# SwiGLU gate by one ScalarE function instead of tangent and a VectorE pass, with scores grouped by four, in a Linformer attention + feed-forward kernel

## The chip, the cores and the metric

The kernel runs on one core of a Trainium2 chip. TensorE (PE) multiplies matrices into PSUM, VectorE (DVE), ScalarE (ACT) and GpSimd (POOL) work on tiles, SyncE (SP) only issues DMAs here. The metric is the device time of one execution in microseconds (us); lower is better. The kernel before took 548.34 us, the median of three runs (547.98 to 548.58).

## The reference

Eight batches, eight heads, 1024 tokens, head size 64. Keys and values are first projected along the sequence from 1024 to 64 rows (E and F), then comes ordinary attention over those 64; its output, 512 wide per token, goes through a gated feed-forward block with 1536 inner columns:

```
k_proj = einsum('ks,bhsd->bhkd', E, k)
v_proj = einsum('ks,bhsd->bhkd', F, v)
attn = softmax(q @ k_proj^T / sqrt(64))
x = (attn @ v_proj)                # tokens x 512
g = x @ w_gate
silu = g * (1 / (1 + exp(-g)))
out = (silu * (x @ w_val)) @ w_out
```

## The kernel before

Tokens are taken in 16 chunks of 512 (two per batch, `c` = 2 * batch + half). A chunk has 12 steps `f`, one for each 128 inner columns. A step is two calls:

- `f_g` (L531): four 128x512 matmuls into a PSUM bank "gps" (two banks take turns), then ScalarE's tangent of half of it into the SBUF tile `th`.
- `f_v` (L537): four matmuls into a bank "vps" (two banks), then two VectorE passes: L541 makes `s1` = (th + 1) * gate, L546 makes `hT` = 0.5 * s1 * value, in bf16. Since x * sigmoid(x) = 0.5 * x * (1 + tanh(x / 2)), this is silu(gate) * value.

The output product of a finished chunk runs during the next chunk: from chunk 1 on as seven half-size products (`f_m`, L666; six 128x256 matmuls each, two products p), with sums of `hT` halves made on POOL and DVE (`h_sum`, L590) and of the results (`m_34`, `m_52`, `m_16`, `m_7`). Chunk 0 uses plain products (`f_y`, L552).

Attention of a batch is made in eight units `u` of 128 tokens by four heads pairwise, while the previous batch's feed-forward runs:

- `u_S` (L354): four 128x128 score matmuls into a bank "sc", then the exponent on ScalarE (L372) into `ee` (four buffers).
- `u_R` (L390): row sums and reciprocals on DVE. `u_N` (L398): normalising on POOL (L409).
- From batch 1 on a DMA on SP's queue transposes four units' weights at once (`u_AD`, L346), as q was before (`u_TD`). Batch 0 transposes on PE instead (`u_T`, `u_A`), with ScalarE or DVE copying the result out of PSUM.
- `u_PVt` (L457) or, for batch 0, `u_PV` (L444) multiplies by the projected values; copies into `xT` feed `f_g` and `f_v`.

The order is written out by hand. The main loop over all 192 steps `t` runs `f_g`, slot 2t, `f_v`, the list `late[t]` (output products and sums), slot 2t + 1. `place(b)` (L725) fills the slots of batch b, relative to s0 = 48 * (b - 1); batch 0's second half is filled at L926 to L931. Each engine follows its own queue in that order and waits on semaphores. Scores take the banks of `psa` ("a", two of them); while c < 2 a third bank ("z") takes part in turns (`bank`, L153). Two units on one slot follow each other on PE with nothing in between.

In the general branch (L774), which runs only when the row sums are out of bounds, the maximum is subtracted first; it does not run here.

```
for t in range(NIT):
    f_g(c, f, i)
    run_slot(2 * t)
    f_v(c, f, i)
    for fn, *a in late.pop(t, ()):
        fn(*a)
    run_slot(2 * t + 1)
```

Of the kernel before, what the change touches and what calls it, by code (L numbers as in the profile page):

```python
# [9 lines left out]
AF = mybir.ActivationFunctionType  # L10
ALU = mybir.AluOpType
AX = mybir.AxisListType
BF16 = mybir.dt.bfloat16
FP32 = mybir.dt.float32
# [8 lines left out]
P = 128  # L23
# [5 lines left out]
CW = 512  # L29
# [10 lines left out]
def kernel(  # L40
# [19 lines left out]
    nc = tc.nc  # L60
    scale = 1.0 / float(D) ** 0.5
# [8 lines left out]
    fw = ctx.enter_context(tc.tile_pool(name="fw", bufs=3))  # L70
# [26 lines left out]
    kb, vb, qb, xT, hT = {}, {}, {}, {}, {}  # L97
# [409 lines left out]
    gp = {}  # L507
# [3 lines left out]
    def f_mm(c, f, w, i=None):  # L511

        if i != 1:


            where = "y" if (c, f, w) == (0, 2, 0) else "gv"[w]
            half[c, f, w] = bank(where, [P, CW], FP32, where + "ps")
        ps = half[c, f, w]
        x = xT[divmod(c, CH)]
        ts = slice(0, CW) if i is None else slice(256 * i, 256 * (i + 1))  # L520
        for kt in range(NKT):
            nc.tensor.matmul(  # L522
                out=ps[:, ts],
                lhsT=(wg, wv)[w][:, kt, f * P : (f + 1) * P],
                rhs=x[:, kt, ts],
                start=(kt == 0),
                stop=(kt == NKT - 1),
            )
        return ps

    def f_g(c, f, i=None):  # L531
        ps = f_mm(c, f, 0, i)
        th = fw.tile([P, CW], FP32, name="th", tag="th")
        nc.scalar.activation(out=th[:], in_=ps[:], func=AF.Tanh, scale=0.5)  # L534
        gp[0] = (ps, th)

    def f_v(c, f, i=None):  # L537
        ps = f_mm(c, f, 1, i)
        g, th = gp.pop(0)
        s1 = fw.tile([P, CW], FP32, name="s1", tag="s1")  # L540
        nc.vector.scalar_tensor_tensor(  # L541
            out=s1[:], in0=th[:], scalar=1.0, in1=g[:], op0=ALU.add, op1=ALU.mult
        )
        if f == 0:
            hT[c] = h_pool.tile([P, NFT, CW], BF16, name="hT", tag="hT")
        nc.vector.scalar_tensor_tensor(  # L546
            out=hT[c][:, f, :], in0=s1[:], scalar=0.5, in1=ps[:], op0=ALU.mult, op1=ALU.mult
        )

    yy = {}  # L550

# [170 lines left out]
    def put(s, fn, *a):  # L722
        slots[s].append((fn, a))

    def place(b):  # L725
        s0 = 48 * (b - 1)
        if b == 1:
            put(22, u_TD, 1, 0)
            put(29, u_K1, 1)
            put(32, u_KT, 1)  # L730
            put(40, u_V1, 1)
            sa = (35, 36, 37, 38, 41, 42, 43, 44)
            put(41, u_AD, 1, 0)
            put(30, u_TD, 1, 1)
            put(47, u_AD, 1, 1)
            put(46, u_PVt, 1, 0, (0, 1), ("aa", "av"))
        else:
            if b == 2:
                put(s0 + 10, u_KV, b)
            else:  # L740
                put(s0 + 8, u_KV, b, "kv", (0, H), "v")
            put(s0 + (13 if b == 2 else 11), u_KT, b)
            put(s0 + (9 if b == 2 else -6), u_TD, b, 0)
            put(s0 + (11 if b == 2 else -4), u_TD, b, 1)
            sa = [s0 + j for j in ((17, 18, 22, 23, 27, 30, 33, 36) if b == 2 else (14, 17, 20, 23, 26, 29, 32, 35))]
            put(sa[3] + 4, u_AD, b, 0)
            put(sa[7] + 4, u_AD, b, 1)
            put(s0 + 44, u_PVt, b, 0, (0, 1), ("aa", "yz"))
        for j in range(NJ):
            put(sa[j], u_S, b, j)  # L750
            put(sa[j] + 1, u_R, b, j)
            put(sa[j] + 1, u_N, b, j)
        put(s0 + (68 if b == 1 else 56), u_PVt, b, 1, (0, 1), ("aa", "yz"))

    def run_slot(s):
# [18 lines left out]
    def general():  # L774
# [6 lines left out]
        with tc.For_i(0, B) as turn, tc.manual_schedule():  # L781
            turn_of.append(turn)
            b = 0
            load_k(b)
            load_v(b)
            u_KV(b)
            u_KT(b)
            for ch in range(CH):
                c = CH * b + ch
                load_q(b, ch)  # L790
                for u in range(4 * ch, 4 * ch + 4):
                    u_T(b, u)
                    u_S(b, u)
                    u_R(b, u)
                    u_N(b, u)
                    u_A(b, u)
                u_PVt(b, ch, (0, 1), ("aa", "yz"))
                for f in range(NFT):
                    f_g(c, f)
                    f_v(c, f)  # L800
                for m in (1, 2, 5, 6, 7):
                    h_sum(c, m, 0, HF, nc.vector)
                for n in range(14):
                    f_m(c, n)

    with tc.manual_schedule():
# [3 lines left out]
        for i in range(2):  # L810
            nc.scalar.dma_start(
                out=kraw[i][:],
                in_=k[0, 2 * i : 2 * i + 2].rearrange("h (p j) d -> p h (j d)", j=NJ),
# [111 lines left out]

        for i, u in enumerate(range(4, 8)):  # L926
            put((12, 12, 13, 14)[i], u_T, 0, u)
            put(13 + i, u_S, 0, u)
            put(14 + i, u_R, 0, u)
            put(14 + i, u_N, 0, u)  # L930
            put((17, 18, 20, 21)[i], u_A, 0, u, nc.scalar)  # L931
        put(19, u_PV, 0, 1, 0)
        put(20, u_PV, 0, 1, 1)
# [5 lines left out]
        for b in range(1, B):  # L939
            place(b)  # L940
        for b in range(2, B):
            s0 = 48 * (b - 1) - (20 if b == 3 else 24)
            at = (43, 43, 44, 45) if b == 2 else (s0, s0 + 2, s0 + 4, s0 + 6)
# [31 lines left out]
        for t in range(NIT):  # L975
            c, f = divmod(t, NFT)
            ring["wide"] = c < 2
            i = 1 if t < 2 else None
# [6 lines that stand above are left out]
# [34 lines left out]
```

## Time and profile before

| what | value |
|---|---|
| median of three runs | 548.34 us |
| the profiled execution's own time | 548.89 us |
| its span, first to last instruction | 547.2 us |
| PE, DVE, ACT, POOL busy | 536.7, 413.7, 232.8, 305.9 us |
| mean granted TensorE clock | 1.000 |
| loads of ScalarE's function table | 1 |

The profile is of one execution. Its groups of instructions give the line, the engine, the operation, what is written from what, the shape and the count, then busy time and the mean length of one in ns, then the idle time of the engine in front of them and what ended it. In the timeline the columns are the start in us, the time covered in us, the engine, the line and the tiles; a bracket holds idle time before and its cause. Neighbouring instructions of one kind are merged into one row.

### The profile page before, as it was taken

Reading aid. Unit: us, or ns where it says so; the run is one execution under the profiler, and the core shown is the slowest. Engines: PE = TensorE matmul, PEld = TensorE weight load, DVE = VectorE, ACT = ScalarE, POOL = GpSimd, SP = SyncE. Lnnn points to the kernel's source line nnn. Section 1 sums busy time; section 2 is a strip of 40 time slices with the busy share of each in tenths; the row PEclk is TensorE's granted clock in tenths of the full one; section 3 lists DMA queues with packets and bytes.
Section 4 is the critical chain, followed back from the end, with each engine's and each line's share of the span. In section 5 each row is a group of like instructions: output and inputs, shape, how many; then the busy total and the mean of one; then the engine's idle time right before and its main releaser. Section 6 shows DMA issues by size and latency. Waiting matters only on the chain.

```text
span 547.2 us, 9550 instructions
## 1 busy us (share of the span) xinstructions
PE 536.7 (98%) x3558; PEld 313.6 (57%) x3558; DVE 413.7 (76%) x702; ACT 232.8 (43%) x416; POOL 305.9 (56%) x428
## 2 busy tenths in 40 slices
PE   7999999999999999999999999999999999999996
PEld 3654445556556555566555665566555655555665
DVE  3687897779668876779677795687857887676883
ACT  3565453353444434344434444434444443443331
POOL 6962395478616864177632966248661666416171
PEclk9999999999999999999999999999999999999999
DMA  9999969929921599008961199512991123101003
GB/s 194 191 195 200 159 147 198 173 78 161 196 67 41 103 191 207 21 21 155 197 148 39 40 154 204 106 40 64 184 202 54 39 78 78 40 38 40 8 32 120
DMA packets 112227, 62.92 MB, mean 115 GB/s; under 512 B 65968, under 2 KB 103856, under 8 KB 112176
## 3 DMA queue, kind: packets, MB, share of 16 engines
q0 software_dynamic: 43952, 29.49, 37.6%
q1 hardware_dynamic: 67392, 31.46, 26.3%
q10 hardware_dynamic: 832, 1.31, 0.8%
q8 instruction: 29, 0.48, 0.4%
q14 instruction: 22, 0.18, 0.1%
HBM read 60.29 MB, written 16.78 MB: 141 GB/s over the span
## 4 chain that ended last, share of the span: by engine, by line
PE 94%; DMA 4%; ACT 0%; issue 0%; DVE 0%; POOL 0%; DVEq 0%; ACTq 0%; POOLq 0%
PE vps L522 31%; PE gps L522 30%; PE yps L624 25%; PE sc L364 2%; DMA wv<-in_moe_w_val_dram 2%; PE kvp L173 2%; PE yps L558 2%; PE pv L468 1%; DMA qb<-in_q_dram 1%; POOL AA L409 0%; PE kvp L212 0%; PE kvp L197 0%; PE qTp L329 0%; PE pv L448 0%; PE yps L522 0%
## 5 line engine op out<-in xcount | busy, mean ns | idle before, releaser
L522 PE MATMUL vps<-xT,wv 128*128 128x512 bf16 (+1 forms) x776 | 197.6, 377 | 0.8 <-DMA wv<-in_moe_w_val_dram 0.8
L534 ACT ACTIVATE th<-gps 128x512 f32<-128x512 f32 x191 | 114.1, 597 | 198.3 <-PE gps L522 196.1
L522 PE MATMUL gps<-xT,wg 128*128 128x512 bf16 (+1 forms) x772 | 196.5, 377 | 0.0
L541 DVE SCALAR_TENSOR_TENSOR s<-th,gps 128x512 f32<-128x512 f32 x191 | 129.3, 677 | 60.7 <-ACT th L534 59.5
L546 DVE SCALAR_TENSOR_TENSOR hT<-s,vps 128x512 bf16<-128x512 f32 x192 | 132.1, 688 | 21.7 <-PE vps L522 1.7
L607 POOL TENSOR_TENSOR hs<-hT 128x256 bf16<-128x256 bf16 x180 | 118.9, 683 | 47.2 <-DVE hT L546 46.6
L522 PEld LDWEIGHTS <-wv 128*128 128x128 bf16 x776 | 73.1, 98 | 85.5 <-issue 6.7
L624 PEld LDWEIGHTS <-hs 128*128 128x128 bf16 x900 | 88.1, 98 | 34.6 <-issue 0.6
L522 PEld LDWEIGHTS <-wg 128*128 128x128 bf16 x776 | 74.0, 98 | 51.4 <-issue 0.2
L654 POOL TENSOR_TENSOR tt<-tt,ysb 128x512 f32<-128x512 f32 x28 | 35.6, 1270 | 106.4 <-DVE tt L653 106.4
L409 POOL TENSOR_TENSOR AAd<-ee,zr 128x512 bf16<-128x512 f32 x56 | 58.5, 1044 | 30.1 <-ACT ee L372 17.6
L624 PE MATMUL yps<-ws,hs 128*128 128x256 bf16 x540 | 68.6, 273 | 0.2 <-DVE ysb L693 0.2
L372 ACT ACTIVATE ee<-sc 128x512 f32<-128x512 f32 x64 | 37.8, 595 | 31.6 <-PE sc L364 30.4
L624 PE MATMUL yps<-ws,hT 128*128 128x256 bf16 x360 | 48.8, 273 | 0.0
L624 PE MATMUL yps<-wo,hs 128*128 128x256 bf16 x360 | 48.6, 273 | 0.1
L643 POOL TENSOR_TENSOR tt<-xs 128x256 f32<-128x256 f32 x30 | 28.1, 937 | 36.7 <-ACT xs L641 36.0
L394 DVE TENSOR_REDUCE zr<-ee 128x8 f32<-128x512 f32 x64 | 43.3, 677 | 5.1 <-ACT ee L372 4.8
L607 DVE TENSOR_TENSOR hs<-hT 128x1536 bf16<-128x1536 bf16 (+1 forms) x49 | 45.2, 928 | 0.1
L624 PEld LDWEIGHTS <-hT 128*128 128x128 bf16 x360 | 35.2, 98 | 16.0
L641 ACT COPY xs<-yps 128x512 f32<-128x512 f32 x30 | 17.6, 586 | 28.0 <-PE yps L624 24.7
L648 ACT COPY ysb<-yps 128x512 f32<-128x512 f32 x30 | 17.6, 586 | 27.5 <-PE yps L624 27.5
L477 ACT CAST xT<-pv 128x512 bf16<-128x512 f32 x56 | 28.8, 599 | 0.0
(108 smaller groups left out, 324.0 us busy)
## 6 DMA issues: line engine op xcount, KB each, us to landing
out_dram<-ysb SPq DMA_DIRECT2D x27, 512.0 KB, 2.7
qb<-in_q_dram POOLq DMA_DIRECT2D x14, 512.0 KB, 17.6
kb<-in_k_dram POOLq DMA_DIRECT2D x7, 1024.0 KB, 10.3
vb<-in_v_dram POOLq DMA_DIRECT2D x7, 1024.0 KB, 15.1
wo<-in_moe_w_out_dram POOLq DMA_DIRECT2D x2, 768.0 KB, 21.4
out_dram<-ysb SPq DMA_DIRECT2D x6, 256.0 KB, 2.4
kraw<-in_k_dram ACTq DMA_DIRECT2D x2, 512.0 KB, 4.9
qb<-in_q_dram POOLq DMA_DIRECT2D x4, 256.0 KB, 8.1
```

Of the source, the lines that this page charges most:

```text
L372: nc.scalar.activation(out=e[:].rearrange("p h j k -> p (h j k)"), in_=ps[:].rearrange("p a k -> p (a k)"), func=AF.Exp, scale=scale,)
L394: nc.vector.reduce_sum(out=z, in_=e[:], axis=AX.X)
L409: eng.tensor_tensor(out=a.rearrange("p j h k -> p h j k"), in0=ee.pop((b, u))[:], in1=r.unsqueeze(3).to_broadcast([P, 4, 2, KP]), op=ALU.mult,
L477: nc.scalar.copy(out=xT[b, ch][:, kt, :], in_=ps[:])
L522: nc.tensor.matmul(out=ps[:, ts], lhsT=(wg, wv)[w][:, kt, f * P : (f + 1) * P], rhs=x[:, kt, ts], start=(kt == 0), stop=(kt == NKT - 1),)
L534: nc.scalar.activation(out=th[:], in_=ps[:], func=AF.Tanh, scale=0.5)
L541: nc.vector.scalar_tensor_tensor(out=s1[:], in0=th[:], scalar=1.0, in1=g[:], op0=ALU.add, op1=ALU.mult)
L546: nc.vector.scalar_tensor_tensor(out=hT[c][:, f, :], in0=s1[:], scalar=0.5, in1=ps[:], op0=ALU.mult, op1=ALU.mult)
L607: eng.tensor_tensor(out=hs[c, m][:, fs, :], in0=quarter(hT[c], *a)[:, fs], in1=quarter(hT[c], *b)[:, fs], op=op,)
L624: nc.tensor.matmul(out=ps, lhsT=lhsT, rhs=ws[m][:, f, :] if rhs is None else rhs, start=(start and f == 0), stop=(f == HF - 1), skip_group ...
L643: nc.gpsimd.tensor_tensor(out=t[:, 0], in0=xs[:, 0], in1=xs[:, 1], op=ALU.add)
L654: nc.gpsimd.tensor_tensor(out=t[:], in0=t[:], in1=yo[c, p][:, 1:3], op=ALU.subtract)
```

## The change

Three parts. The gate: ScalarE takes x * sigmoid(x) of the gate's bank straight, in place of the tangent; the first VectorE pass is gone and the second becomes a plain product of `th` and the value bank. The bank of the gate is thereby read by ScalarE alone. The new function and the exponent stand in different tables of ScalarE, and a table load comes wherever the two follow each other. The slots: the units of a batch stand in groups, two on one slot and two on the next, with no gate on ScalarE's queue inside a group of four. `u_AD` is at slots 27 and 39 as numbers of their own (before: four after the fourth and eighth unit, the same slots, but 40 in place of 39 in batch 2). `u_R` and `u_N` follow on slots of their own.

```
     def f_g(c, f, i=None):
         ps = f_mm(c, f, 0, i)
         th = fw.tile([P, CW], FP32, name="th", tag="th")
-        nc.scalar.activation(out=th[:], in_=ps[:], func=AF.Tanh, scale=0.5)
-        gp[0] = (ps, th)
+        nc.scalar.activation(out=th[:], in_=ps[:], func=AF.Silu)
+        gp[0] = th
 
     def f_v(c, f, i=None):
         ps = f_mm(c, f, 1, i)
-        g, th = gp.pop(0)
-        s1 = fw.tile([P, CW], FP32, name="s1", tag="s1")
-        nc.vector.scalar_tensor_tensor(
-            out=s1[:], in0=th[:], scalar=1.0, in1=g[:], op0=ALU.add, op1=ALU.mult
-        )
+        th = gp.pop(0)
         if f == 0:
             hT[c] = h_pool.tile([P, NFT, CW], BF16, name="hT", tag="hT")
-        nc.vector.scalar_tensor_tensor(
-            out=hT[c][:, f, :], in0=s1[:], scalar=0.5, in1=ps[:], op0=ALU.mult, op1=ALU.mult
-        )
+        nc.vector.tensor_tensor(out=hT[c][:, f, :], in0=th[:], in1=ps[:], op=ALU.mult)
...
-            sa = (35, 36, 37, 38, 41, 42, 43, 44)
+            sa = (36, 36, 37, 37, 42, 42, 43, 43)
             put(41, u_AD, 1, 0)
...
-            sa = [s0 + j for j in ((17, 18, 22, 23, 27, 30, 33, 36) if b == 2 else (14, 17, 20, 23, 26, 29, 32, 35))]
-            put(sa[3] + 4, u_AD, b, 0)
-            put(sa[7] + 4, u_AD, b, 1)
+            sa = [s0 + j for j in ((18, 18, 19, 19, 28, 28, 29, 29) if b == 2 else (16, 16, 17, 17, 28, 28, 29, 29))]
+            put(s0 + 27, u_AD, b, 0)
+            put(s0 + 39, u_AD, b, 1)
             put(s0 + 44, u_PVt, b, 0, (0, 1), ("aa", "yz"))
         for j in range(NJ):
             put(sa[j], u_S, b, j)
-            put(sa[j] + 1, u_R, b, j)
-            put(sa[j] + 1, u_N, b, j)
+            at = sa[j] + 1 + (j % 4 if b > 1 else j % 4 // 2)
+            put(at, u_R, b, j)
+            put(at, u_N, b, j)
...
         for i, u in enumerate(range(4, 8)):
             put((12, 12, 13, 14)[i], u_T, 0, u)
-            put(13 + i, u_S, 0, u)
-            put(14 + i, u_R, 0, u)
-            put(14 + i, u_N, 0, u)
+            put((13, 13, 15, 15)[i], u_S, 0, u)
+            put((14, 14, 16, 16)[i], u_R, 0, u)
+            put((14, 14, 16, 16)[i], u_N, 0, u)
             put((17, 18, 20, 21)[i], u_A, 0, u, nc.scalar)
```

## The prediction

> **What bounds the kernel now.** I read the page first: the busy line, the clock row and the chain that ended last.
>
> ```profile
> PE 536.7 (98%) x3558; PEld 313.6 (57%) x3558; DVE 413.7 (76%) x702; ACT 232.8 (43%) x416; POOL 305.9 (56%) x428
> ...
> PEclk9999999999999999999999999999999999999999
> ...
> PE 94%; DMA 4%; ACT 0%; issue 0%; DVE 0%; POOL 0%; DVEq 0%; ACTq 0%; POOLq 0%
> ```
>
> TensorE is busy 98% of the span, at full clock, and is 94% of the chain; DVE and ACT are 0% of it. Busy time could hide slow matmuls, so I looked at the timeline of PE alone, in the middle of the kernel:
>
> ```profile
> 237.06 0.39 PE L364 MATMUL sc<-BD,qTd 128*128 128x128 bf16 x4
> 237.28 1.03 PE L522 MATMUL gps<-xT,wg 128*128 128x512 bf16 x4
> 238.15 1.03 PE L522 MATMUL vps<-xT,wv 128*128 128x512 bf16 x4
> 239.01 0.82 PE L624 MATMUL yps<-wo,hs 128*128 128x256 bf16 x6
> 239.66 1.03 PE L522 MATMUL gps<-xT,wg 128*128 128x512 bf16 x4
> ```
>
> From start to start, four score matmuls take 0.22 us, four 512-wide ones 0.86, six 256-wide ones 0.65, so a step of gate, value and one output product takes 0.86 + 0.86 + 0.65 = 2.37. The row after each group starts as its predecessor's issue ends: nothing is lost. The 96 to 320 us stretch says the same (224.00 of 224.00 us busy in the view by stretches). So a cheaper DVE can gain nothing here, and **any wait put on PE is added whole to the end**. The question is what ACT's new work does to PE.
>
> **What is removed, and what it is worth.** The groups of instructions:
>
> ```profile
> L534 ACT ACTIVATE th<-gps 128x512 f32<-128x512 f32 x191 | 114.1, 597 | 198.3 <-PE gps L522 196.1
> L541 DVE SCALAR_TENSOR_TENSOR s<-th,gps 128x512 f32<-128x512 f32 x191 | 129.3, 677 | 60.7 <-ACT th L534 59.5
> L546 DVE SCALAR_TENSOR_TENSOR hT<-s,vps 128x512 bf16<-128x512 f32 x192 | 132.1, 688 | 21.7 <-PE vps L522 1.7
> L372 ACT ACTIVATE ee<-sc 128x512 f32<-128x512 f32 x64 | 37.8, 595 | 31.6 <-PE sc L364 30.4
> ```
>
> The pass at L541 goes: 192 x 0.677 = 130 us of DVE. All of it lies beside PE. In PE's list of waits DVE appears only for opening work (zeros 1.4, BD 0.7, kb 0.2) and at the tail (ysb 0.2). One more place shows in the timeline: the third tile's value matmuls could issue at 25.15 + 0.86 = 26.01 but wait for the first product.
>
> ```profile
> 25.47 0.69 DVE L546 SCALAR_TENSOR_TENSOR hT<-s,vps 128x512 bf16<-128x512 f32 x1
> 26.21 1.02 PE L522 MATMUL vps<-xT,wv 128*128 128x512 bf16 x4
> ```
>
> Without L541 that product ends near 25.75, even with a table load ahead of the first gate (it starts at 24.39 instead of 24.04): **gain 0.2**. At the tail PE's 0.15 to 0.3 us gaps follow ACT and DVE work on output products, not hT: 0. The product at L546 becomes a two-operand multiply; the nearest row, L659 (a sum of the same size out of PSUM), takes 681 against 688 ns: 0. The new function is not in the trace; the rows for exponent, tangent and copy of this shape lie at 595, 597 and 586, so 0.60 +- 0.01: 0.
>
> **What is added.** Tangent and exponent needed one table load for the whole kernel. In the built order of the changed kernel, ACT has 34 loads in the part that runs: one in front of every group of exponents and one in front of the next gate. The row of the one load before (ACT's groups):
>
> ```profile
> L161 ACT ACT_TABLE_LOAD x1 | 1.3, 1283 | 2.0 <-issue 2.0
> ```
>
> 33 x 1.283 = 42 us more on ACT, 43% busy becoming about 49%. That alone costs nothing; what matters is who waits. The load of a group stands behind the wait for its first scores, and the gate tile of the same step is in front of it, so it cannot run early.
>
> *Batches 2 to 7: 12 groups of four.* PE's new order is gate, scores 1 and 2, value, one output product (six matmuls), scores 3 and 4, next gate. Only two PSUM banks ("a") hold scores here, so scores 3 wait for exponent 1, and scores 4 for exponent 2. Before, the units stood three or more slots apart and no such wait is listed. Time 0 is the end of issue of the gate's matmuls. ACT starts a gate 0.20 after that (237.28 + 0.87 = 238.15, then the second line), and neighbours on ACT start 0.49 apart (third and fourth):
>
> ```profile
> 237.48 0.60 ACT L372 ACTIVATE ee<-sc 128x512 f32<-128x512 f32 x1 [1.14 <-PE sc L364]
> 238.35 0.60 ACT L534 ACTIVATE th<-gps 128x512 f32<-128x512 f32 x1 [0.27 <-PE gps L522]
> ...
> 240.73 0.60 ACT L534 ACTIVATE th<-gps 128x512 f32<-128x512 f32 x1 [0.23 <-PE gps L522]
> 241.22 0.59 ACT L372 ACTIVATE ee<-sc 128x512 f32<-128x512 f32 x1
> ```
>
> - ACT: gate 0.20 to 0.80, load to 2.08, exponent 1 to 2.68, exponent 2 from 2.57 to 3.17.
> - PE: scores 1, 2 to 0.45; value to 1.31; product to 1.96. Scores 3 may go at 2.68 + 0.05 (26.16 to 26.21 above is such a handover) = 2.73: **stall 0.77**. They end at 2.95; scores 4 go at 3.22: **0.27**.
> - Later: exponents end at 4.24, the second load at 5.52, the next gate at 6.12. Its PSUM bank is wanted two steps after, at 3.44 + 2 x 2.37 = 8.2, the value bank (free at 6.9) at 9.1. That wait stays hidden, with 2 us to spare.
>
> 1.04 x 12 = **12.5 us**.
>
> *Batch 1: two groups.* Three banks take turns here, so only scores 4 wait for exponent 1. With four 512-wide output matmuls in between they arrive at 2.40: 0.33. In the second group eight lie between, 3.26: none. **0.3**.
>
> *Batch 0, second half (33 to 46 us): two groups of two*, among copies of q and of the transposed weights on ACT, with four loads on ACT's one queue. Followed from 33.11 with old clock times. ACT's second q copy ends at 34.88 and scores 2 now come before the next transpose: wait 0.3. Load 34.88 to 36.16, exponents to 37.26; the transpose that reuses the first scores' bank waits for the first exponent: 0.5. q copy to 37.75, load to 39.03, gate to 39.63, last q copy to 40.12: scores 4, ready to issue at 38.17, go at 40.18: 2.0. Load to 41.40, exponents to 42.50, load to 43.78, gate, copy, gate, copy to 45.88: the first weights-times-values matmul, ready at 44.32, goes at 45.95, where before it lost 0.1 at most: 1.5. After it PE's waits are covered again. **4.3**.
>
> *Moved, without cost.* The sums, reciprocals and POOL's normalising move with the units: on DVE 0.677 + 0.203 each, covered by the pass that left; on POOL 1.04 + 0.27 each, by 44% idle. From batch 3 the fourth normalising of the first half comes three slots earlier (21 for 24), so SP's transposing DMA behind it starts sooner, not later; its place in SP's queue is the same (one moves by a slot in batch 2). Its landing in time is not new. POOL's loads of k, v and q keep their slots.
>
> Sum: 12.5 + 0.3 + 4.3 - 0.2 = 16.9. The profiled execution took 548.89 us (span 547.2 and 1.7 around it): 565.8; from the median of the three runs, 548.34, 565.2. Forecast **566**.
>
> **The price in doubt** is what a load holds up. Below: if it overlaps its neighbours by 0.1 at either end as ACTIVATEs do (0.60 long, 0.49 apart), each group loses 0.2 less and batch 0 some 0.8: 562. Above: if emptying and refilling the engine costs a whole ACTIVATE, 0.60, per load, groups lose 7.2 more, batch 1 0.7, batch 0 (four loads in one chain) 2.4: 576. I take the row's own length, 1.28. A change of 0.2% (1.1 us) is about what a measurement of this kernel can tell.
>
> [...]
>
> **Rivals.**
> - *Not slower: the load holds nothing.* At a visible price of L, exponent 1 ends at 0.80 + L + 0.60; scores 3 arrive at 1.96. Below L = 0.5 us the 12 groups cost nothing, batch 0 keeps its 0.3 for the q copy and the head gains 0.2: 549.0. For it: ACT is 57% idle, and PE has other work for 1.5 us. Against: 1283 ns stand in the row, as engine time. Chance 5%, most of it within 0.2%.
> - *The load costs more than its row*, 0.60 or beyond: 576 and up. For it: ACTIVATEs overlap, so a switch has something to empty. Against: ACT began its load at 1.98 directly after two DMA issues, and a record usually holds the whole hold-up. 20%, of which some 8% over 578.
> - *Less than 1.0 per group*: exponents or scores meet more luckily, or batch 0 is less tight than my chain of copies: 555 to 560. For it: the old order shows slack on ACT nearly everywhere. Against: every handover used is from a row. 5%.
> - The forecast's own range, 560 to 571: 70%.
>
> Together 560 to 578 holds 70 + 12 = 82%. Faster by over 0.2%: 2%; within: 3%; slower: 95%.
>
> **What would show it.** Right: ACT_TABLE_LOAD x34 with about 1283 ns; DVE about 50% busy; PE waits "sc <- ACT ee" 24 times near 0.8 and 0.3; a PE gap of 2 us near 38 and of 1.5 near 44; PE's busy time nearly unchanged while the span grows. Wrong: ACT idle of over 0.2 us directly behind loads (dearer), scores without waits (cheaper), or a wait of gps for ACT or DVE (my 2 us of cover is gone).

## The result, and the profile after

The changed kernel takes **566.58 us** (median of 4 runs, 566.35 to 566.84) against 548.36 (4 runs): a ratio of 1.0333, 95% interval 1.0315 to 1.0351. Forecast was 566, in a range of 560 to 578. The page of the profiled execution, with the row that stands where L541 and L546 stood:

```profile
span 565.2 us, 9374 instructions
...
PE 541.8 (96%) x3558; PEld 314.3 (56%) x3558; DVE 289.7 (51%) x510; ACT 273.5 (48%) x449; POOL 304.1 (54%) x428
...
PE 84%; ACT 8%; DMA 3%; POOL 2%; issue 2%; DVE 0%; ACTq 0%; POOLq 0%; DVEq 0%
...
L542 DVE TENSOR_TENSOR hT<-th,vps 128x512 bf16<-128x512 f32 x192 | 131.7, 686 | 213.3 <-PE vps L522 186.8
```

DVE lost 124 us of work, ACT gained 41, and the span grew by 18. PE does the same 3558 matmuls; its busy time (536.7 us before, 541.8 now) grew because the modelled ends of matmuls reach into the new waits (in the group shown below by 0.17 and 0.26 us; 12 x 0.43 = 5.2). ACT, which stood at 0% of the chain before, holds 8% of it. The groups of ACT, and what PE waited for:

```profile
L534 ACT ACTIVATE th<-gps 128x512 f32<-128x512 f32 x191 | 114.0, 597 | 217.0 <-PE gps L522 213.7 <-DVE BD L285 1.9 <-DVE hT L542 1.2
...
L534 ACT ACT_TABLE_LOAD x17 | 21.8, 1283 | 0.3
L372 ACT ACT_TABLE_LOAD x16 | 20.5, 1283 | 0.3
```

```profile
PE sc L364 <- ACT ee L372: 7.8, 13, 0.6
PE sc L364 <- ACT qT L161: 1.9, 1, 1.9
PE pv L448 <- ACT AT L161: 1.5, 1, 1.5
...
PE yps L618 <- ACT xT L477: 0.8, 1, 0.8
```

The gate costs what the tangent did (597 ns); each of the 33 added loads is 1283 ns long. In the list of waits (total, times, longest) the scores wait 13 times for an exponent: the 12 groups of batches 2 to 7 and one of batch 1. The prediction looked for 24; the short waits of scores 4 lie within the modelled end of the matmul before and so are not in the list. Here is one such group in the timeline (start, time covered; a bracket is idle time before, counted from the modelled end of the matmul before):

```profile
244.88 0.61 PE L364 MATMUL sc<-BD,qTd 128*128 128x128 bf16 x8
...
245.08 0.60 ACT L534 ACTIVATE th<-gps 128x512 f32<-128x512 f32 x1 [0.22 <-PE gps L522]
245.33 1.03 PE L522 MATMUL vps<-xT,wv 128*128 128x512 bf16 x4
...
245.70 1.28 ACT L372 ACT_TABLE_LOAD   x1
246.19 0.82 PE L618 MATMUL yps<-wo,hs 128*128 128x256 bf16 x6
...
246.99 2.15 ACT L372 ACTIVATE ee<-sc 128x512 f32<-128x512 f32 x4
...
247.64 0.87 PE L364 MATMUL sc<-BD,qTd 128*128 128x128 bf16 x8 [0.63 <-ACT ee L372]
248.35 1.03 PE L522 MATMUL gps<-xT,wg 128*128 128x512 bf16 x4
```

Read it from 244.88, the end of the gate's issue. The load starts 0.02 after the gate's record ends, the exponents 0.01 after the load. PE is through with the output product at 246.19 + 0.65 = 246.84 and issues scores 3 at 247.64: 0.80 (the bracket, counted from the modelled end, has 0.63). From there to the next gate are 0.71 where eight score matmuls take 0.45: 0.26 for scores 4. Together 1.06; forecast 0.77 + 0.27.

The starts of the value matmuls of the same step in both timelines show where the 17.9 us of span came from:

| stretch | forecast | measured |
|---|---|---|
| up to the third tile | -0.2 | -0.5 |
| batch 0, second half | 4.3 | 4.3 |
| batch 1 | 0.3 | 0.4 |
| batch 2 | 2.1 | 3.4 |
| batches 3 to 7 | 10.4 | 10.55 |
| tail | 0 | -0.1 |

0.2 of the first row is the wait that was forecast to go; the rest is the landing of the first loads, which differs from run to run by about 1 us (that row is -0.3 for the slots alone, where the gate is the old one, and -1.2 for the gate alone and for everything at once). The largest error, batch 2, is a step that I left out:

```profile
115.85 0.91 PE L468 MATMUL pv<-AT,VS 64*64 64x512 bf16 x8
...
116.11 1.28 ACT L534 ACT_TABLE_LOAD   x1
...
117.41 0.60 ACT L534 ACTIVATE th<-gps 128x512 f32<-128x512 f32 x1
...
117.90 2.05 ACT L477 CAST xT<-pv 128x512 bf16<-128x512 f32 x4
...
118.53 1.47 PE L618 MATMUL yps<-ws,hs 128*128 128x256 bf16 x12 [0.80 <-ACT xT L477]
```

Batch 1's weights-times-values products stand one step behind batch 2's first group. They need the banks of the exponents (0.3 lost), and their copies out of PSUM stand on ACT behind the group's second load; the output product needs those banks (0.8 by the bracket, 0.96 from start to start).

### The profile page after: what moved, and what is told of

The parts are those of the page before. It is cut to its first block, busy times and chain, and to the rows that moved or that the text cites. A ratio compares the mean times of both kernels' runs of the same rounds, so it can differ in the third digit from the quotient of the medians.

```text
span 565.2 us, 9374 instructions
## 1 busy us (share of the span) xinstructions
PE 541.8 (96%) x3558; PEld 314.3 (56%) x3558; DVE 289.7 (51%) x510; ACT 273.5 (48%) x449; POOL 304.1 (54%) x428
## 4 chain that ended last, share of the span: by engine, by line
PE 84%; ACT 8%; DMA 3%; POOL 2%; issue 2%; DVE 0%; ACTq 0%; POOLq 0%; DVEq 0%
PE gps L522 28%; PE vps L522 26%; PE yps L618 23%; ACT ee L372 3%; ACT L372 3%; PE kvp L173 2%; PE yps L552 2%; PE sc L364 2%; DMA qb<-in_q_dram 1%; DMA Fraw<-in_F_dram 1%; PE pv L468 1%; ACT th L534 1%; POOL wv L136 1%; POOL wg L136 0%; POOL qb L126 0%
## 5 line engine op out<-in xcount | busy, mean ns | idle before, releaser
L542 DVE TENSOR_TENSOR hT<-th,vps 128x512 bf16<-128x512 f32 x192 | 131.7, 686 | 213.3 <-PE vps L522 186.8
L637 POOL TENSOR_TENSOR tt<-xs 128x256 f32<-128x256 f32 x30 | 23.2, 774 | 50.4 <-ACT xs L635 50.4
L372 ACT ACTIVATE ee<-sc 128x512 f32<-128x512 f32 x64 | 34.6, 597 | 0.9 <-PE sc L364 0.4
L364 PE MATMUL sc<-BD,qTd 128*128 128x128 bf16 x224 | 19.1, 218 | 9.0 <-ACT ee L372 7.8
```

The costliest lines, as they stand in the source:

```text
L364: nc.tensor.matmul(out=ps[:, slot, :], lhsT=t[:, n, :], rhs=BD[b % 2][:, 4 * g + n, :], start=True, stop=True)
L372: nc.scalar.activation(out=e[:].rearrange("p h j k -> p (h j k)"), in_=ps[:].rearrange("p a k -> p (a k)"), func=AF.Exp, scale=scale,)
L542: nc.vector.tensor_tensor(out=hT[c][:, f, :], in0=th[:], in1=ps[:], op=ALU.mult)
L637: nc.gpsimd.tensor_tensor(out=t[:, 0], in0=xs[:, 0], in1=xs[:, 1], op=ALU.add)
```

## The experiments

My theory: loads beside PE are free, and the loss is the sum of a few named waits. The rivals: ACT's extra 42 us cost PE time by one wait or another, wherever it is relieved; or the grouping costs, not the load.

**Gate alone** (the diff's first two hunks; all units in their slots of before).

> The new gate, but every unit of scores in its slot of before. The built order then has 114 table loads in the part that runs, against 34 in the changed kernel and 1 before. Theory (time is lost only where PE stands still for ACT; loads beside PE are free): ACT's work in a stretch of units becomes about 4.25 us for each unit and its one and a half steps (two loads 2.57, an exponent 0.55, gates 0.85, copies 0.25), against 3.8 us of PE, so ACT falls back by some 0.5 us per unit; some 3 us of that are covered by PSUM banks, the rest is 2 to 3 us per batch for six batches, about 6 in batch 1 and 7 in batch 0: 576 us, between 568 and 590. Rival (the grouping itself is what costs, loads are mostly hidden): less than the 566.6 of the changed kernel, near 552.

Measured 577.2 us, ratio 1.0512 (1.0494 to 1.0529). The sum fits, its parts do not. By the starts of the value matmuls batch 0 lost 8.9, batch 1 6.7, batch 2 6.0, batches 3 to 7 only 8.4 (1.65 each): more than expected early, less later. The early parts hold the four places where the granted clock fell (last section). At up to 1.7 us each they are up to 7 of the 28.8 us that the span grew, and the expectation had no such term: that the sum fits is partly luck. PE's waits in this run:

```profile
PE yps L618 <- ACT xs L635: 4.9, 5, 1.0
PE pv L468 <- ACT ee L372: 4.1, 2, 2.1
PE sc L364 <- ACT qT L161: 2.4, 1, 2.4
PE yps L552 <- ACT ysb L561: 2.4, 2, 1.4
```

No scores wait for exponents now, but output products wait for copies that stand behind loads. So 80 more loads than in the changed kernel cost 10.6 us net, the falls of the clock included, and all of the loss lies in batches 0 to 2; in the five late batches it is the faster of the two (1.65 against 2.1). The rival is out: grouping gains over the whole kernel.

**Slots alone** (the changed kernel with the gate of before).

> The grouped slots with the gate of before (tangent and two VectorE passes), so one table load. Theory (the wait of scores 3 and 4 comes from the load in front of exponent 1): without the load exponent 1 ends 1.3 us after the gate's matmuls and scores 3 arrive at 1.96, so the 12 groups cost nothing; 0.3 us are left for the second copy of q in batch 0: 548.7 us, between 548.2 and 549.3. Rival (pairs of units back to back on two banks cost by themselves): 550 to 560.

Measured 555.5 us, ratio 1.0123 (1.0106 to 1.0139): **missed**. The scores do not wait, as expected, but this does:

```profile
PE yps L624 <- DVE tt L653: 5.4, 5, 1.4
```

```profile
262.73 0.63 DVE L541 SCALAR_TENSOR_TENSOR s<-th,gps 128x512 f32<-128x512 f32 x1
...
263.47 0.69 DVE L546 SCALAR_TENSOR_TENSOR hT<-s,vps 128x512 bf16<-128x512 f32 x1
264.07 0.41 DVE L653 TENSOR_TENSOR tt<-tt,yps 128x256 f32<-128x256 f32 x1
...
264.54 0.82 PE L624 MATMUL yps<-ws,hs 128*128 128x256 bf16 x6 [1.00 <-DVE tt L653]
```

With row sums bunched and two passes per step, DVE reaches the sum at L653 late, and the next output product writes into the bank it reads. By the starts of the value matmuls this wait costs 6.2 us over batches 2 to 6; in the next run, with one pass and nearly no waits of scores for exponents, it costs 1.7. So the pass removed was worth nothing in the order of before but is worth some 4.5 us in the new one (an estimate from these two): "covered by the pass that left" was true, and it was needed. The rival "pairs cost by themselves" is right in its number and wrong in its place: no bank of scores is involved.

**Other banks for scores 3 and 4.**

```
-            put(sa[j], u_S, b, j)
+            put(sa[j], u_S, b, j, "aazv"[j % 4] if b > 1 else "a")
```

> The changed kernel, but from batch 2 on scores 3 of a group go to the bank z and scores 4 to a bank of vps, so that neither waits for an exponent; the 34 table loads stay. Theory (the bank is the wait): 1.05 us less in 11 of the 12 groups; not in the first group of batch 2, where the copies into xT stand behind ACT's second load and the output product waits for their banks either way: 566.6 - 11.6 = 555.0 us, between 553.5 and 556.5, and no more PE waits of sc for ee from batch 2 on. Rival (ACT's extra 42 us is what PE waits for, by one wait or another): 562 to 567, the wait turning up at gps or vps.

Measured 556.8 us, ratio 1.0154 (1.0135 to 1.0173), 9.8 under the changed kernel with the same 34 loads. Each of the 11 groups gives back 1.06, as expected; but the second group of each of batches 2 to 6 then loses 0.34 again, 1.7 in all, to the wait seen in the run before, now small:

```profile
PE yps L618 <- ACT xT L477: 1.5, 1, 1.5
...
PE yps L618 <- DVE tt L647: 0.9, 5, 0.2
...
PE sc L364 <- ACT ee L372: 0.2, 1, 0.2
```

The first group of batch 2 gained nothing: its wait moved to the copies, 1.5 where 0.8 stood. The bank was the wait; the rival's 562 to 567 is out.

**Batch 0's second half as one group.**

```
-            put((12, 12, 13, 14)[i], u_T, 0, u)
-            put((13, 13, 15, 15)[i], u_S, 0, u)
-            put((14, 14, 16, 16)[i], u_R, 0, u)
-            put((14, 14, 16, 16)[i], u_N, 0, u)
-            put((17, 18, 20, 21)[i], u_A, 0, u, nc.scalar)
+            put((12, 12, 13, 13)[i], u_T, 0, u)
+            put((14, 14, 15, 15)[i], u_S, 0, u, "aaav"[i])
+            put((15, 15, 16, 16)[i], u_R, 0, u)
+            put((15, 15, 16, 16)[i], u_N, 0, u)
+            put((19, 20, 21, 22)[i], u_A, 0, u, nc.scalar)
...
+        put(22, u_PV, 0, 1, 0)
+        put(22, u_PV, 0, 1, 1, nc.vector)
+        put(23, u_PV, 0, 1, 2)
+        put(23, u_PV, 0, 1, 3, nc.vector)
```

> The changed kernel, but the second half of batch 0 with its four units as one group: scores on slots 14, 14, 15, 15, the fourth in a bank of vps, transposes of q a little earlier, transposes of the weights on slots 19 to 22 and their products on 22 and 23. 32 table loads in place of 34. Theory (batch 0 loses 4.3 us because four loads and the copies lie in one chain on ACT's queue): 0.3 to 0.6 of the 4.3 are left, 562.7 us, between 562 and 563.5. Rival (batch 0 loses its time elsewhere, the chain was only argued): 566 to 567.

Measured 562.8 us, ratio 1.0260 (1.0243 to 1.0277): 3.8 less than the changed kernel. By the starts of the value matmuls the second half of batch 0 loses 0.9 where it lost 4.3, so 3.4 of the 3.8 are its own, a little less than expected, and the rest lies at the head and the tail. Left are waits of 0.5 for a gate and 0.2 for a copy.

**Everything at once**: the two edits above (in batch 1 "aaav"), the first group of batch 2 on slots 16 and 17, and the last two row sums of a batch one slot later.

```
-            at = sa[j] + 1 + (j % 4 if b > 1 else j % 4 // 2)
+            at = sa[j] + 1 + (j % 4 + (j > 5) if b > 1 else j % 4 // 2)
```

> The changed kernel with every wait that was found taken away: scores 3 and 4 of a group in the banks z and vps (batch 1: scores 4 in a bank of vps), batch 0's second half as one group, the first group of batch 2 two slots earlier, so that the products of the weights of batch 1 no longer stand right behind it, and the last two row sums of the second group a slot later, behind the sum that the output product waits for. 32 table loads stay, 40 us of ACT. Theory (loads cost only through these waits): 0.7 us left in batch 0, 0.2 won at the head: 548.9 us, between 548.0 and 550.0. Rival (some of the 18 us belongs to the loads themselves): over 551.

Measured 549.0 us (11 runs), ratio 1.0015 (1.0006 to 1.0024), with 32 loads. What is left:

```profile
PE gps L522 <- ACT th L534: 0.5, 1, 0.5
PE pv L468 <- ACT ysb L642: 0.5, 1, 0.5
PE pv L485 <- ACT BDV L254: 0.2, 1, 0.2
PE gps L522 <- DVE xT L161: 0.2, 1, 0.2
```

Over batches 3 to 7, with 20 of the loads, the value matmuls lose nothing net. Behind the third tile this profile loses 1.6 us, 0.9 of it in batch 0 and the rest up to the first group of batch 2; at the head it is 1.2 ahead of the profile before by the landing of the first loads and the 0.2 of the third tile. So the loads cost nothing beyond their waits that these runs can tell: 40 us of them lie beside PE. No version here beats the kernel before.

**A second load in front of each group.**

```
+        if b > 1 and u % 4 == 0:
+            nc.scalar.activation(out=junk[:], in_=junk_in[:], func=AF.Sqrt)
         nc.scalar.activation(
```

> The changed kernel with one more table switch in front of each group of exponents from batch 2 on: a square root of a 128x1 tile of ones, whose result is not used. 46 loads. Theory (every microsecond that ACT is later with exponent 1 is one of PE's): a load of 1.28 and some 0.2 for the tiny function, 1.5 us for each of 12 groups: 584.6 us, between 582 and 587, with scores 3 waiting 2.1 us and scores 4 0.3 as before. Rival (a switch costs more than its row, as an emptied engine would): more than 2 us per group, over 590.

Measured 594.0 us, ratio 1.0828 (1.0812 to 1.0845): 27.4 more than the changed kernel, **missed** by 9.4. The two expectations are told apart by the timeline of two groups of one batch. The first:

```profile
255.44 0.82 PE L622 MATMUL yps<-wo,hs 128*128 128x256 bf16 x6
...
258.40 0.87 PE L366 MATMUL sc<-BD,qTd 128*128 128x128 bf16 x8 [2.15 <-ACT ee L376]
259.11 1.03 PE L526 MATMUL gps<-xT,wg 128*128 128x512 bf16 x4
```

Scores 3 wait 258.40 - 256.09 = 2.31, that is 1.51 more than 0.80: load 1.283 and the small function 0.203, as expected. No switch here costs more than its row. The second group waits as long, and then:

```profile
276.81 0.87 PE L366 MATMUL sc<-BD,qTd 128*128 128x128 bf16 x8 [2.15 <-ACT ee L376]
277.51 1.78 PE L526 MATMUL gps<-xT,wg 128*128 128x512 bf16 x4
...
279.09 1.91 PE L526 MATMUL vps<-xT,wv 128*128 128x512 bf16 x4
280.80 0.95 PE L622 MATMUL yps<-wo,hs 128*128 128x256 bf16 x6
```

The same four matmuls cover 1.78 and 1.91 in place of 1.03. In the view by stretches (busy time of PE, PEld, DVE, ACT, POOL, then the clock) of a first and a second group:

```profile
255.00:261.00 6.00, 3.75 (x27) 2.21 (x26) 2.33 (x5) 5.94 (x8) 4.01 (x7) 1.00 0.00 0
```

```profile
276.00:282.00 6.00, 5.04 (x23) 2.46 (x24) 2.54 (x6) 4.42 (x8) 3.33 (x5) 0.72 1.24 205
```

The granted clock fell to 0.72 over those 6 us, and so it did at 133, 205, 348, 420 and 491 us: behind one wait per batch. 12 x 1.51 = 18.1 for the loads leaves 27.4 - 18.1 = 9.3, or 1.6 for each fall. The expectation had no term for the clock; that is what it missed, and the rival, though the time lies in its range, is out: the price of the switch is 1.51.

**Late batches spread again** (batches 3 to 7 in their slots of before, batches 0 to 2 grouped).

> The changed kernel, but batches 3 to 7 with their units in the slots of before (one unit every three slots), batches 0 to 2 grouped. 94 loads in place of 34. Theory (loads beside PE are free while ACT keeps up): as in the run with the gate alone, 1.65 us per batch in place of 2.1, so 2.3 us less: 564.3 us, between 563 and 565.5, with no waits of sc for ee in these batches. Rival (fewer loads are always better): 570 and more.

Measured 564.0 us, ratio 1.0283 (1.0268 to 1.0299): 2.5 under the changed kernel, with 60 loads more. The waits per batch are now 1.0 and 0.3 of another kind:

```profile
PE yps L618 <- ACT xs L635: 4.9, 5, 1.0
...
PE gps L522 <- ACT th L534: 1.5, 5, 0.3
```

## Why the prediction was right

- *PE is the bound, and any wait put on it is added whole*: right. That the rows of the table add up to the growth of the span follows from how they are read; what shows it is that taking the waits away gives all but 0.7 us of it back (549.0).
- *The pass at L541 is worth nothing but 0.2*: right for the order of before. The slots alone showed that the new order lives on it.
- *Load of 1283 ns, gate 0.60, product 0.68*: 1283, 597, 686. The price in doubt was the row's own length, shown twice: in the group (0.02 and 0.01 at its ends) and by the second load (1.51, of which 1.283 + 0.203 are the two records).
- *"The load costs more than its row", 0.60 per load or beyond (576 and up)*: out. The load starts 0.02 us after the gate's record ends and the exponent 0.01 us after the load's, so neither emptying nor refilling is to be seen beside the 1283 ns.
- *1.04 per group, 12 groups*: 1.06. *Batch 1, 0.3*: 0.4. *Batch 0, 4.3, by the chain of copies and four loads*: 4.3, and 3.4 of it goes with that chain.
- *"Later: ... That wait stays hidden, with 2 us to spare"*: right for 11 groups (gates wait for ACT nowhere in the list), wrong for the first of batch 2. That step followed only the next gate behind the second load. The products of batch 1's weights and their copies into `xT` behind that gate were left out there; they cost 1.2.
- The total came out closer than its parts: 1.2 missed in batch 2 stands against 0.3 of luck with the first loads and rounding up from 565.8.

Not tried: a kernel with the last 1.2 us of waits taken out of the one with everything at once; whether it would beat the kernel before is open.

## What to carry to other kernels

When one engine is full, read another engine's extra work not as busy time but as lateness: follow the queue behind each inserted instruction to the first wait of the full engine, and compare the lateness with the other work that it has until then. Some 40 us of table loads cost 18 us or 0.7, by which PSUM bank a tile is given and what copy stands behind a load. An engine's relief can be worth next to nothing in one order of work (0.2 us in that of before, by its rows) and several us in another (some 4.5, the estimate from the slots alone and the other banks), so an order and the work that it needs are to be tried together and apart.

## What was not expected of the hardware

A wait of some 2.15 us (as the profile counts it) was followed by matmuls at half speed for a time (1.71 us for four value matmuls, 279.09 to 280.80, where the changed kernel's group has 0.86, 245.33 to 246.19), at a cost of 1.6 us, in one group of each batch and not in the other, though both waits are alike (clock 0.72 and 1.00 over 6 us). In the run with the gate alone the same fall (0.72 to 0.76 over 6 us, four times) came around waits of 2.04 to 2.44 us; the first row is the third of them. The changed kernel's longest wait in mid-work, 1.9, shows no fall: its granted clock is 1.00 from 30 to 52 us, the second row.

```profile
90.00:96.00 6.00, 3.91 (x17) 1.40 (x13) 3.15 (x5) 5.91 (x9) 5.98 (x8) 0.72 1.12 165
```

```profile
30.00:52.00 22.00, 18.11 (x118) 9.31 (x117) 9.62 (x17) 17.43 (x27) 10.83 (x18) 1.00 1.34 198
```

Shorter stretches of the second-load run bound the fall behind its second group:

```profile
272.00:276.00 4.00, 2.66 (x22) 1.62 (x20) 2.40 (x3) 3.73 (x5) 1.78 (x3) 1.00 0.98 136
276.00:280.00 4.00, 3.09 (x15) 1.37 (x15) 1.64 (x4) 3.92 (x7) 2.12 (x4) 0.71 1.23 204
280.00:284.00 4.00, 3.95 (x23) 2.30 (x23) 2.78 (x5) 1.47 (x3) 1.57 (x3) 0.87 1.25 208
284.00:288.00 4.00, 4.00 (x27) 2.42 (x25) 2.81 (x6) 0.60 (x1) 3.31 (x5) 1.00 1.42 197
```

The clock is 1.00 in the first and the last; in the two between, 4 x 0.29 + 4 x 0.13 = 1.7 us of matmul time are lost, near the 1.6 found from the times. The falls of that run lie a batch apart: the six stretches of 6 us with 0.72 begin at 133, 205, 276, 348, 420 and 491 us. With the gate alone the four stretches begin at 38, 45, 90 and 128 us, at no equal distances. What sets off a fall, and why it follows one of two like waits and not the other, is not shown here.
